# Matmuls with discarded results inside the last inverse transform and ahead of the first transposes

## The chip, the cores and the metric

The kernel runs on one core of a Trainium2 chip. The metric is the time of one execution on the device in microseconds. The engines are named as the profile names them: PE is TensorE (PEld its weight loads), ACT is ScalarE, DVE is VectorE, POOL is GpSimd, and SP issues most of the DMAs.

## The reference

A sequence of 2,048 positions with 640 channels passes two blocks, each modulated by vectors that come from `silu(c) @ w_mod`.

```python
h = layernorm(x) * (1 + ca) + sa
kv = shift_conv(k) * v                       # 4 taps along the sequence
y = causal_conv(kv, ssm_k) + kv * ssm_D      # the reference uses an FFT of length 4096
x = x + ga * (h * y)
h = layernorm(x) * (1 + cb) + sb
g = gelu(layernorm(h) @ w1)                  # w1 is 640 x 640
h1 = h + shift_quarters(g) @ w2              # quarters moved by +1, -1, +2, -2 positions
out = x + gb * (h1 + gelu(layernorm(h1) @ w3) @ w4)   # w3, w4: inner width 1728
```

All inputs and the output are bfloat16. The long convolution reaches over the whole sequence. The rest works position by position, apart from the small shifts ahead of w2.

## The kernel before, in words

The long convolution is done as a transform in matmuls. The 4,096-point transform is split in two stages (L408 and L425), once for the filter and once for `kv`. A product in the frequency domain and two inverse stages follow: `inverse1` (L617, L618) with the 128x128 matrices EA and EB, and `inverse2` (L658).

The sequence is held as 16 tiles of 128 positions. A tile A holds the positions whose remainder modulo 64 is 4A to 4A+3, so a position's neighbours in the sequence lie in the same tile or in the next one. `inverse2` takes groups of two or three tiles: [0,1,2], [3,4], [5,6,7], [8,9,10], [11,12,13] and [14,15]. For each tile it makes 32 small matmuls, 32 rows by 32 columns of the array with 160 moving columns each: four row blocks j4, four column blocks cg, and two accumulation steps cpp. Row blocks 0 and 1 go to the first PSUM slot of the group, 2 and 3 to the second. One task stands for the whole group, and two evacuations, on ACT (L209) or DVE (L211), copy the two slots to `y_all`.

Each tile then goes through `chain_a` (multiply by the modulated query, residual, sums for the layernorm), `chain_b` (the second block's layernorm and modulation) and `chain_c` (the inner layernorm and a transpose). The square sums are on ACT (L726). The reciprocal square roots are on POOL (L709, L712). The transpose is done in `turn`: for the first tiles on PE (L769, five 128x128 blocks into a PSUM slot `ps_tr`, which ACT L775 or DVE L777 copies out), and for all others as a DMA transpose issued by SP (L762). `pe_c` and `pe_m` set which: ten tiles go through PE, five ahead of w1 and five ahead of w3. `mm_w1` (L815, L825), `mm_w2` (L870), `mm_w3` (L904) and `mm_w4` (L934, L925) are the four matrix products, and each is evacuated by ACT (gelu) or DVE.

The order of all work is fixed. The kernel records about 1,075 tasks, and the string `ORDER` lists them with their engine and, for PE tasks, the PSUM slot or slots (four slots of 4 KB a partition). The engines then get their instructions in that order, each a queue that is worked off first to last. The groups of `inverse2` stand in PE's order as [0,1,2], two tasks of `silu(c) @ w_mod` (L483), [3,4], [14,15], [5,6,7], [8,9,10], the first tile's transposes, [11,12,13], and then the first w1 product. The cost figures in the calls of `add` were for a planner that made `ORDER`; with `ORDER` given they change nothing. An entry such as `498P:01` places task 498, the group [3,4], on PE with the slots 0 and 1.

Of the kernel before, what the change touches and what calls it, by code (L numbers as in the profile page):

```python
# [9 lines left out]
F32 = mybir.dt.float32  # L10
# [71 lines left out]
class Planner:  # L82
# [9 lines left out]
    def add(self, eng, cost, fn, r=(), w=(), lat=0.0, alloc=None, use=None, after=(), kb=0.0, rate=330.0, port=0.0, act=1.0, ni=0):  # L92
        t = Task()
        t.no = len(self.tasks)
        t.eng, t.cost, t.fn, t.lat, t.kb, t.rate, t.port, t.act, t.ni = eng, cost, fn, lat, kb, rate, port, act, ni
        t.alloc, t.frees = (() if alloc is None else alloc if isinstance(alloc, tuple) else (alloc,)), use
        deps = set(after)
        for acc, wr in [(a, False) for a in r] + [(a, True) for a in w]:
            reg, lo, hi = acc[:3]
            grp = acc[3] if len(acc) > 3 else None  # L100
            lst = self.acc.setdefault(reg, [])
            keep = []
            for e in lst:
                elo, ehi, ewr, egrp, et = e
                if elo < hi and lo < ehi and (wr or ewr) and not (wr and ewr and grp is not None and grp == egrp):
                    deps.add(et)
                if wr and grp is None and lo <= elo and ehi <= hi:
                    continue
                keep.append(e)
            self.acc[reg] = keep  # L110
        for acc, wr in [(a, False) for a in r] + [(a, True) for a in w]:
            self.acc[acc[0]].append((acc[1], acc[2], wr, acc[3] if len(acc) > 3 else None, t))
        deps.discard(t)
        t.deps = deps
        t.succ = []
        t.on = None
        for d in deps:
            d.succ.append(t)
        self.tasks.append(t)
        return t  # L120
# [18 lines left out]
def kernel(  # L139
# [4 lines left out]
    nc = tc.nc  # L144
# [11 lines left out]
    add = pl.add  # L156
# [5 lines left out]
    T01 = mem.tile([P, 20480], BF, name="T01")  # L162
    R3 = mem.tile([P, 20480], BF, name="R3")
    R5 = mem.tile([P, 20560], BF, name="R5")
    RG = mem.tile([P, 8192], BF, name="RG")
    RH = mem.tile([P, 4096], BF, name="RH")
# [30 lines left out]
    def ca(n):  # L197
        return 0.17 + 0.00083 * n
# [7 lines left out]
    def evac(dst, src, n, ps, w, eng=("ACT", "DVE")):  # L206
        def f(e):
            if e == "ACT":
                nc.scalar.copy(dst, src(ps.tile))  # L209
            else:  # L210
                nc.vector.tensor_copy(dst, src(ps.tile))  # L211
        return add(eng, {"ACT": ca(n), "DVE": cd(n)}, f, (), w, use=ps)

    def pst(ps, shape=None, dt=F32, name="ps"):
        if ps.tile is None:
            ps.tile = psA.tile(shape or [P, 2, 512], dt, name=name, tag="q" + ps.place)
        return ps.tile
# [119 lines left out]
    for kb in range(2):  # L337
# [9 lines left out]
        else:  # L347
# [3 lines left out]
            r=[wk[:3]], w=[wk], port=0.4)  # L351
# [9 lines left out]
        r=[("skT", 0, 1)], w=[("RQ", 0, 2560)], port=0.5)  # L361
# [72 lines left out]
    def dep(t, *on):  # L434
        for o in on:
            if o not in t.deps:
                t.deps.add(o)
                o.succ.append(t)

    for b in range(ND):  # L440
        add(("POOL", "DVE"), {"POOL": 0.2, "DVE": 0.16}, lambda e, b=b: eng_of[e].tensor_tensor(sT[:, b, 0:1], sT[:, b, 0:1], Dcol[:, b:b + 1], ALU.add),
            r=[("Dcol", 0, 1)], w=[("Ra", 2048 * b, 2048 * b + 2048)])
# [121 lines left out]
    for js in range(4):  # L564
        for jd in range(4):
            dma(("SP", "POOL"), 64, lambda q, js=js, jd=jd: q.dma_start(RH[32 * jd:32 * jd + 32, 1024 * js:1024 * js + 1024], RK[32 * js:32 * js + 32, 3072:4096]),
                r=[("RK", 3072, 4096)], w=[("RH", 1024 * js, 1024 * js + 1024, "h")], rate=215.0)
# [26 lines left out]
    EAf, EBf = (E[:].rearrange("p c n -> p (c n)") for E in (EA, EB))  # L594
# [41 lines left out]
    for g in range(4):  # L636
        dma("SP", 60, lambda q, g=g: q.dma_start(w2_sb[32 * g:32 * g + 32, 4, :], B_w2[160 * g + P:160 * g + 160, :]), w=[("RG", 3200, 6400, "w2")])
    add("POOL", 0.8, lambda e: nc.gpsimd.tensor_copy(w1x.rearrange("p b (g r) -> p b g r", g=4), w1_sb.rearrange("p b (g r) -> p b g r", g=4)[:, :, :, P:160]),
        r=[("RG", 0, 3200)], w=[("RG", 6400, 7040)])
# [6 lines left out]
    def inverse2(tilesA):  # L646
        n = len(tilesA)
        pss = [Slot() for _ in range(2)]

        def f(e):  # L650
            for s in pss:
                pst(s, name="ps_i2")
            for a, A in enumerate(tilesA):
                for j4 in range(4):
                    for cg in range(4):
                        n1 = 4 * A + cg
                        for cpp in range(2):
                            nc.tensor.matmul(pss[j4 // 2].tile[32 * cg:32 * cg + 32, j4 % 2, a * 160:(a + 1) * 160],  # L658
                                             lhsT=Hs[32 * j4:32 * j4 + 32, n1, cpp, :],
                                             rhs=Zb[32 * j4:32 * j4 + 32, cpp * 64 + n1, :, :],  # L660
                                             start=(cpp == 0), stop=(cpp == 1), tile_position=(32 * j4, 32 * cg))
        t1 = add("PE", 0.38 * n, f, r=[("T01", 0, 20480), ("RH", 0, 4096)], alloc=tuple(pss), act=0.2, ni=64 * n)
        yv = y_all[:, tilesA[0]:tilesA[0] + n, :].rearrange("p a (j u) -> p j a u", j=4)
        for i in range(2):
            t2 = evac(yv[:, 2 * i:2 * i + 2], lambda t: t[:, :, 0:160 * n].rearrange("p j (a u) -> p j a u", a=n), 320 * n, pss[i],
                      [("Rb", D * tilesA[0], D * (tilesA[0] + n), "y")])
            dep(t2, t1)
# [91 lines left out]
    def turn(dT, dk, src, sk, i, pe):  # L759

        if not pe:
            add("SP", 1.3, lambda e: nc.sync.dma_start_transpose(dT[:, :, i * P:(i + 1) * P], src), r=[sk], w=[dk + ("t",)], lat=1.6)  # L762
            return
        ps = Slot()

        def f(e):
            pt = pst(ps, [P, 2, 8, P], BF, name="ps_tr")
            for b in range(ND):
                nc.tensor.transpose(pt[:, 0, b, :], src[:, b * P:(b + 1) * P], ident)  # L769
        t0 = add("PE", 0.29, f, r=[sk, ("RG", 7680, 7808)], alloc=ps, act=0.2, ni=10)  # L770

        def f(e):
            o, x = dT[:, :, i * P:(i + 1) * P], ps.tile[:, 0, 0:ND, :]
            if e == "ACT":
                nc.scalar.copy(o, x)  # L775
            else:
                nc.vector.tensor_copy(o, x)  # L777
        t1 = add(("ACT", "DVE"), {"ACT": ca(640), "DVE": 0.47}, f, w=[dk + ("t",)], use=ps)
        dep(t1, t0)

    def chain_c(g, rn):
        hT, hTk = hnT[g % 3]
        for i, A in enumerate(CG[g]):
            hn, hk = hnr[A % 4]
            normed(hn, hk, h_all[:, A, :], hk_(A), rn, i)
            turn(hT, hTk, hn, hk, i, g < pe_c)
# [73 lines left out]
    def mm_w2(g):  # L860
        for t in MG[g]:
            ps = Slot()
            ix = m_idx[t]

            def f(e, ps=ps, t=t):
                pt = pst(ps, name="ps_w2")
                for fb in range(5):
                    for hf in range(2):
                        c0 = 64 + P * t - (32 * SH[fb] if fb < 4 else 0)
                        nc.tensor.matmul(pt[:, hf, 0:320], lhsT=gsf[:, fb, c0:c0 + P], rhs=w2_sb[:, fb, 320 * hf:320 * hf + 320],  # L870
                                         start=(fb == 0), stop=(fb == 4))
            r = [("gs", max(0, t - 1), min(NT, t + 2)), ("gx", t + 1, t + 2)]
            if t in (0, NT - 1):
                r += [("gpad", 0, 2)]
            t0 = add("PE", 1.37, f, r=r + [("RG", 3200, 6400)], alloc=ps, ni=20)
            hv = h_all[:, t, :].rearrange("p (a n) -> p a n", a=2)
            t1 = add("DVE", 0.82, lambda e, ps=ps, hv=hv, ix=ix: nc.vector.scalar_tensor_tensor(  # L877
                hv, ps.tile[:, :, 0:320], 1.0, hv, ALU.mult, ALU.add, accum_out=stat[:, 2, 0, ix:ix + 1]),
                w=[hk_(t), ("s1", 200 + ix, 201 + ix)], use=ps)
            dep(t1, t0)  # L880
            square_sum(h_all[:, t, :], hk_(t), 2, ix)
        rn = ln_finish(2, m_idx[MG[g][0]], len(MG[g]), g < quick_m)
        xT, xTk = xnT[g % 3]
        for i, t in enumerate(MG[g]):
            xn, xnk = xnr[m_idx[t] % 3]
            normed(xn, xnk, h_all[:, t, :], hk_(t), rn, i)
            turn(xT, xTk, xn, xnk, i, g < pe_m)
# [80 lines left out]
    def last_tile(t, pss, ta, tb):  # L968
# [6 lines left out]
        for hf, td in ((0, ta), (1, tb)):  # L975
# [6 lines left out]
            for cg in range(4):  # L982
                qe = ("SP", "ACT")[cg % 2] if hf else "SP"
                add(qe, 0.45, lambda e, cg=cg, qe=qe, c=c: (nc.sync if qe == "SP" else nc.scalar).dma_start(out_pos[4 * t + cg][:, c], o[32 * cg:32 * cg + 32, c]),
                    r=[oh], lat=1.6)

    inverse2([0, 1, 2])
    inverse2([3, 4])
    gs_zero()
    rest = [[5, 6, 7], [8, 9, 10], [11, 12, 13], [14, 15]]  # L990
    for tl in rest:
        inverse2(tl)
# [69 lines left out]
```

## Time and profile before

| | |
|---|---|
| median of 3 runs | 309.21 us (309.16 to 311.48) |
| profiled execution, its own time | 308.55 us |
| its span, first to last instruction | 306.6 us |
| mean granted PE clock | 0.956 |
| PE busy | 273.5 us (89%), 2,926 matmuls |
| DVE busy | 218.9 us (71%) |
| ACT busy | 210.4 us (69%) |
| POOL busy | 115.4 us (38%) |
| L658, the small matmuls of `inverse2` | 102.3 to 119.6 us of the span |
| L769, transposes on PE | 117.3 to 158.3 us, 50 matmuls |

The profile is of one execution. All its times are counted from the span's start, in microseconds. The row of PE's clock gives the share of full speed that was granted in each of 40 slices of 7.7 us. An idle time is shown with what ended it: the instruction on another engine that released the wait, or "issue" where the profile shows nothing that was waited for. The starts of matmuls are measured, and their ends are modelled.

### The profile page before, as it was taken

Reading aid. Unit: us, or ns where it says so; the run is one execution under the profiler, and the core shown is the slowest. Engines: PE = TensorE matmul, PEld = TensorE weight load, DVE = VectorE, ACT = ScalarE, POOL = GpSimd, SP = SyncE. Lnnn points to the kernel's source line nnn. Section 1 sums busy time; section 2 is a strip of 40 time slices with the busy share of each in tenths; the row PEclk is TensorE's granted clock in tenths of the full one; section 3 lists DMA queues with packets and bytes.
Section 4 is the critical chain, followed back from the end, with each engine's and each line's share of the span. In section 5 each row is a group of like instructions: output and inputs, shape, how many; then the busy total and the mean of one; then the engine's idle time right before and its main releaser. Section 6 shows DMA issues by size and latency. Waiting matters only on the chain.

```text
span 306.6 us, 7417 instructions
## 1 busy us (share of the span) xinstructions
PE 273.5 (89%) x2926; PEld 206.6 (67%) x2926; DVE 218.9 (71%) x430; ACT 210.4 (69%) x359; POOL 115.4 (38%) x257
## 2 busy tenths in 40 slices
PE   0999999996899757877999989999999899999992
PEld 0655556753888535856888767688867777897761
DVE  8999999999999998887689763924759135032342
ACT  4789999988689789998896686376643673542100
POOL 5898075052113698544337521424113130300000
PEclk9999999999799955599999999999999999999997
DMA  6999999669799942502800240222420402151112
GB/s 206 268 179 186 222 181 258 165 171 257 198 255 290 281 109 66 239 2 45 287 6 0 25 80 18 53 50 48 40 63 4 86 2 48 25 68 34 43 48 58
DMA packets 58163, 35.74 MB, mean 117 GB/s; under 512 B 39872, under 2 KB 54848, under 8 KB 58128
## 3 DMA queue, kind: packets, MB, share of 16 engines
q1 hardware_dynamic: 56896, 31.81, 44.8%
q0 software_dynamic: 1136, 3.41, 4.2%
q8 instruction: 23, 0.38, 0.5%
q14 instruction: 12, 0.10, 0.1%
q10 hardware_dynamic: 96, 0.04, 0.1%
HBM read 16.31 MB, written 2.62 MB: 62 GB/s over the span
## 4 chain that ended last, share of the span: by engine, by line
PE 50%; DVE 14%; ACT 10%; POOL 10%; DMA 7%; issue 6%; SPq 0%; ACTq 0%; POOLq 0%; DVEq 0%
PE ps_w L934 13%; PE ps_w L904 13%; PE ps_s L425 5%; PE ps_w L870 4%; PE ps_s L408 4%; PE ps_ksh L457 4%; POOL lnv L712 3%; DMA R<-RK 3%; PE ps_w L815 3%; DVE Rb L606 3%; DMA RG<-R 3%; ACT RG L726 2%; ACT R L209 2%; DVE Rb L395 2%; DMA Ra<-in_A_ssm_k_dram 1%
## 5 line engine op out<-in xcount | busy, mean ns | idle before, releaser
L904 PE MATMUL ps_w<-R,T 128*128 128x256 bf16 (+1 forms) x630 | 64.0, 261 | 0.0
L904 PEld LDWEIGHTS <-T 128*128 128x128 bf16 x630 | 55.8, 98 | 7.4 <-issue 1.3
L934 PE MATMUL ps_w<-T,R 128*128 128x320 bf16 x416 | 59.0, 299 | 0.0
L934 PEld LDWEIGHTS <-R 128*128 128x128 bf16 x416 | 40.3, 98 | 15.4 <-issue 0.3
L908 ACT ACTIVATE R<-ps_w 128x1024 bf16<-128x1024 f32 (+2 forms) x36 | 28.9, 826 | 28.6 <-PE ps_w L904 28.5
L726 ACT ACTIVATE RG<-R 128x640 bf16<-128x640 bf16 x32 | 23.5, 734 | 18.5 <-DVE R L753 10.1
L209 ACT CAST T<-ps_s 128x1024 bf16<-128x1024 f32 x33 | 31.6, 1025 | 3.5 <-PE ps_s L408 3.4
L957 DVE TENSOR_TENSOR T<-ps_w,R 128x640 bf16<-128x640 f32 x15 | 12.3, 822 | 27.7 <-PE ps_w L934 16.5
L408 PE MATMUL ps_s<-F1bd,Rb 128*128 128x256 bf16 x160 | 22.9, 295 | 8.8 <-DVE Rb L395 8.4
L408 PEld LDWEIGHTS <-Rb 128*128 128x128 bf16 x160 | 16.6, 106 | 15.0 <-DVE Rb L395 9.0
L877 DVE SCALAR_TENSOR_TENSOR R<-ps_w,R 128x640 bf16<-128x640 f32 x16 | 13.0, 818 | 17.8 <-PE ps_w L870 14.7
L209 ACT CAST R<-ps_s 128x640 bf16<-128x640 f32 x37 | 23.4, 722 | 1.9 <-PE ps_s L425 1.8
L617 PE MATMUL ps_i<-EA,Rb 128*128 128x128 bf16 x160 | 20.6, 227 | 3.1 <-DVE Rb L606 2.7
L712 POOL TENSOR_TENSOR lnv<-lnv,mhalf 128x2 f32<-128x2 f32 (+1 forms) x29 | 22.5, 776 | 2.3
L870 PE MATMUL ps_w<-RG,R 128*128 128x320 bf16 x160 | 23.1, 299 | 0.0
L425 PE MATMUL ps_s<-T,RG 64*128 64x320 bf16 x256 | 22.3, 297 | 0.3 <-ACT R L209 0.2
L209 ACT CAST T<-ps_i 128x1024 bf16<-128x1024 f32 x20 | 19.1, 1021 | 4.9 <-PE ps_i L618 4.8
L618 PE MATMUL ps_i<-EB,Rb 128*128 128x128 bf16 x160 | 20.4, 227 | 1.4 <-DVE Rb L606 1.4
L815 PE MATMUL ps_w<-R,RG 128*128 128x256 bf16 (+1 forms) x200 | 21.5, 273 | 0.0
L211 DVE CAST R<-ps_s 128x640 bf16<-128x640 f32 x27 | 20.7, 818 | 0.9 <-ACT R L209 0.2
L815 PEld LDWEIGHTS <-RG 128*128 128x128 bf16 x200 | 18.7, 110 | 1.6 <-issue 0.2
L711 POOL TENSOR_TENSOR lnv<-stat,lnv 128x2 f32<-128x2 f32 x19 | 5.5, 291 | 37.1 <-ACT RG L726 36.5
(173 smaller groups left out, 522.7 us busy)
## 6 DMA issues: line engine op xcount, KB each, us to landing
Ra<-in_A_ssm_k_dram SPq DMA_DIRECT2D x5, 512.0 KB, 5.5
Ra<-in_A_q_dram SPq DMA_DIRECT2D x8, 320.0 KB, 5.8
R<-in_w_mod_dram SPq DMA_DIRECT2D x6, 400.0 KB, 8.0
out_dram<-RH SPq DMA_DIRECT2D x60, 40.0 KB, 1.6
T<-in_B_w_dram SPq DMA_DIRECT2D x1, 2160.0 KB, 8.3
T<-in_B_w_dram SPq DMA_DIRECT2D x1, 2080.0 KB, 10.2
RH<-in_w_mod_dram SPq DMA_DIRECT2D x4, 400.0 KB, 5.1
RK<-R POOLq DMA_DIRECT2D x5, 256.0 KB, 5.1
```

Source lines behind the costliest of these rows:

```text
L209: nc.scalar.copy(dst, src(ps.tile))
L211: nc.vector.tensor_copy(dst, src(ps.tile))
L408: nc.tensor.matmul(psv[:, ml, :], lhsT=xL[:, s0:s0 + P], rhs=F1r, start=True, stop=True)
L425: nc.tensor.matmul(psv[:, g], lhsT=Gs[p, k, 64 - 64 * cc:192 - 64 * cc], rhs=T1b[p, cc * 32 + k], start=(cc == 0), stop=(cc == 1), tile_po ...
L617: nc.tensor.matmul(psv[:, w, :], lhsT=Av[:, r_, :, g_], rhs=EAf, start=True, stop=False)
L712: nc.gpsimd.tensor_tensor(rs, rs, mhalf[:, 0:n], ALU.pow)
L726: add("ACT", 0.74, lambda e: nc.scalar.activation(junk, src, ACT.Square, scale=float(D) ** -0.5, accum_out=stat[:, li, 1, t:t + 1]), r=[sk ...
L815: nc.tensor.matmul(pt[:, fb, 0:cw], lhsT=w1_sb[:, b, 160 * fb:160 * fb + P], rhs=hT[:, b, 0:cw], start=(b == 0), stop=(b == ND - 1))
L870: nc.tensor.matmul(pt[:, hf, 0:320], lhsT=gsf[:, fb, c0:c0 + P], rhs=w2_sb[:, fb, 320 * hf:320 * hf + 320], start=(fb == 0), stop=(fb == 4))
L904: nc.tensor.matmul(pt[:, fl, 0:cw], lhsT=w3_sb[:, b, fb * P:(fb + 1) * P], rhs=xT[:, b, 0:cw], start=(b == 0), stop=(b == ND - 1))
L908: nc.scalar.activation(g3[g % 2][:, f0:f0 + fn, 0:cw], ps.tile[:, 0:fn, 0:cw], ACT.Gelu_apprx_tanh)
L934: nc.tensor.matmul(bank(i, hf), lhsT=gg[:, fb, i * P:(i + 1) * P], rhs=w4_sb[:, fb, 320 * hf:320 * hf + 320], start=(fb == 0 and i == 0), ...
```

## The change

In `inverse2`, after row blocks j4 = 0, 1 and 2 of each tile, one matmul is added with all 128 rows and columns of the array: weights EA, moving data from T01, results into the last quarter of the group's second PSUM slot, from column 160 a to 512 for the a-th tile of the group. Row block 3 of the same tile and of the later tiles overwrites those columns, so nothing of the result is used. These are 48 matmuls with 512, 352 or 192 moving columns. In `turn`, on the PE path, three matmuls of 512 columns with the weights EA go to the unused half of the transposes' PSUM slot, ahead of the five transposes. These are 30 for the ten tiles. The recorded reads grow by what the new matmuls read. `ORDER` stays as it is, and so do the order of all other instructions on every engine and the number of instructions on the engines other than PE.

```diff
+                    if j4 < 3:
+                        nc.tensor.matmul(pss[1].tile[:, 1, 160 * a:512], lhsT=EAf, rhs=T01[:, 160 * a:512], start=True, stop=True)
-        t1 = add("PE", 0.38 * n, f, r=[("T01", 0, 20480), ("RH", 0, 4096)], alloc=tuple(pss), act=0.2, ni=64 * n)
+        t1 = add("PE", 0.38 * n, f, r=[("T01", 0, 20480), ("RH", 0, 4096), ("E", 0, 1)], alloc=tuple(pss), act=0.6, ni=70 * n)
...
             pt = pst(ps, [P, 2, 8, P], BF, name="ps_tr")
+            spare = pt[:, 1].rearrange("p b n -> p (b n)").bitcast(F32)
+            for _ in range(3):
+                nc.tensor.matmul(spare, lhsT=EAf, rhs=RG[:, 0:512], start=True, stop=True)
             for b in range(ND):
                 nc.tensor.transpose(pt[:, 0, b, :], src[:, b * P:(b + 1) * P], ident)
-        t0 = add("PE", 0.29, f, r=[sk, ("RG", 7680, 7808)], alloc=ps, act=0.2, ni=10)
+        t0 = add("PE", 0.29, f, r=[sk, ("RG", 7680, 7808), ("RG", 0, 512), ("E", 0, 1)], alloc=ps, act=0.2, ni=16)
```

## Prediction

> **What bounds the kernel now.** First the page's slices of the span and the total waits of TensorE (PE):
>
> ```profile
> PE   0999999996899757877999989999999899999992
> ...
> PEclk9999999999799955599999999999999999999997
> PE ps_i L658 <- issue: 5.3, 3, 1.9
> PE ps_tr L769 <- DVE RK L721: 2.6, 3, 1.4
> ```
>
> One stretch, slices 14 to 17, has little PE work and half a clock; the 32x32 matmuls of the last inverse (L658) lie there and stand idle three times, with no releaser in the trace. Next the order of PE's work there (start, duration, idle before it):
>
> ```profile
> 102.34 1.21 PE L658 MATMUL ps_i<-T,RH 32*32 32x160 bf16 x96
> 103.48 1.53 PE L483 MATMUL ps_mod<-R,silu_w 128*128 128x320 bf16 x10
> 104.94 0.35 PE L658 MATMUL ps_i<-T,RH 32*32 32x160 bf16 x16
> 105.45 0.29 PE L658 MATMUL ps_i<-T,RH 32*32 32x160 bf16 x2 [0.16 <-DVE Rb L211]
> 107.43 2.34 PE L658 MATMUL ps_i<-T,RH 32*32 32x160 bf16 x128 [1.68 <-issue]
> 111.43 2.10 PE L658 MATMUL ps_i<-T,RH 32*32 32x160 bf16 x128 [1.67 <-issue]
> 115.43 1.00 PE L658 MATMUL ps_i<-T,RH 32*32 32x160 bf16 x46 [1.91 <-issue]
> 117.33 0.71 PE L769 MATMUL ps_tr<-RG,RK 128*128 128x128 bf16 x5 [0.89 <-DVE RK L721]
> 117.97 1.64 PE L658 MATMUL ps_i<-T,RH 32*32 32x160 bf16 x96
> 119.54 2.31 PE L815 MATMUL ps_w<-R,RG 128*128 128x128 bf16 x20
> ...
> 148.34 0.44 PE L769 MATMUL ps_tr<-RG,RH 128*128 128x128 bf16 x5
> ```
>
> A tile has 32 of these matmuls, so the groups can be counted off: tiles [0,1,2] at 102.34; [3,4] from 104.94 to 108.00; then [14,15], [5,6,7], [8,9,10] until 116.43; [11,12,13] at 117.97. The idle times come after exactly 128 weight-load and matmul pairs, 256 instructions, and PE resumes every 4.00 us: it waits for its instructions.
>
> What waits for these groups is ScalarE (ACT), which empties their PSUM (L209). Its queue in order of time:
>
> ```profile
> 108.00 1.29 ACT L209 CAST Rb<-ps_i 128x640 bf16<-128x640 f32 x2 [0.99 <-PE ps_i L658]
> 109.91 1.28 ACT L209 CAST Rb<-ps_i 128x640 bf16<-128x640 f32 x2
> 116.47 0.96 ACT L209 CAST Rb<-ps_i 128x960 bf16<-128x960 f32 x1 [0.26 <-PE ps_i L658]
> 120.71 2.66 ACT L209 CAST Rb<-ps_i 128x960 bf16<-128x960 f32 x3
> 123.39 1.28 ACT L817 ACT_TABLE_LOAD   x1
> ```
>
> From 120.71 to 135.2 ACT has only gaps of 0.2 us, none of them put down to PE, and the chain of waits runs through it. Before that (110.17 to 118.9) the chain is GpSimd's (POOL) layernorm steps, first released by ACT's square sum, which is queued behind the 108.00 evacuation. So an inverse group that ends later is felt, and a faster matmul between 117 and 129 us, where every consumer is late anyway, is not. From 145.6 us on PE is full except for two DMA-transpose waits of 0.94 (183.45) and 0.89 (241.71).
>
> **The skill.** "TensorEngine Tiling (Array Packing)", Key Properties: changing the tiling mode drains the engine. The trace agrees and prices it: the 26 matmuls of L934 from 169.88 start every 0.136, so the last starts at 173.28, and the 64-row one behind it at 173.51: 0.23, or 0.095 more. From the last 32x32 start of the first group (103.32) to the full-array one at 103.48 it is 0.160: 160 columns (0.067) and 0.093. At half clock the same step before 119.54 takes 0.269, some 0.136 more than the columns.
> "TensorE: Matmul & The Clock Gate", What's actually happening: a 3,413 ns free-running window judges activity; an idle one halves the clock, a busy one restores it. Narrow stretches of the table by stretch show half clock from 108.8 to 129.27, six such windows. Same page, Back-to-back issue gap: columns over 2.4 GHz plus 2.5 ns; the 0.136 for 320 columns agrees.
> "Runtime: NRT & Kernel Launch", Instruction fetch mechanics: refills come in blocks of 256 instructions and are mostly hidden. The block size agrees; hidden they are not (5.3 us).
>
> **Part 1: 48 matmuls within the inverse groups.** After row blocks 0 to 2 of each tile stands one 128x128 matmul of 512, 352 or 192 columns (first, second, third tile of the group). Each changes the mode twice. One costs columns/2.4 + 0.19 us: 0.40, 0.34, 0.27; thrice each, 1.2, 1.0, 0.8. So a group of three tiles takes 1.14 + 3.0 = 4.15, one of two 0.76 + 2.2 = 3.0. Bounds of the unseen mixture: no drain at all (1.3 and 1.1 per group), or twice the drain. I take the measured drain, because three kinds of pairs show the same 0.095.
> Now the walk, each step as time before -> after:
> - [0,1,2] ends 103.5 -> 106.5; the ten w_mod matmuls behind it 104.9 -> 108.0.
> - [3,4]: its instructions are there at 107.43, so the first fetch wait vanishes under the delay. Ends 108.0 -> 111.0 (+3.0). ACT's evacuation, the square sum behind it and POOL's 110.17 step move as much. VectorE's own half of the first group (104.25) moves by 2.3 and is no later than that.
> - [14,15] ends at 114.0, ACT wanted it at 109.91 + 3.0: ACT now +4.1.
> - [5,6,7] ends at 118.1, ACT wants it at 114.41 + 4.1 = 118.5: nothing. A block of instructions now lasts over 4 us, so the other two fetch waits are gone too; without that cover this would be 3.6 worse.
> - [8,9,10] ends at 122.3, ACT wants it at 116.47 + 4.1 = 120.6: ACT +5.9.
> - the first transposes with their extras (0.75) until 123.4, then [11,12,13] until 127.7; ACT wants it at 120.71 + 5.9 = 126.6: ACT +7.0.
> From there ACT is in order and full, and the transposes on DMA that PE waits for at 145.61 come out of it: +7.0. The extras also write the second PSUM slot from the first block on instead of the third; it is free by then in each group (the slot's evacuations are the ACT rows above).
>
> **Part 2: 30 matmuls of 512 columns ahead of ten tiles' transposes.** They do not read the tile that the transposes wait for, only the weights and a free slot. Three take 3 x 0.216 = 0.65, with no mode change. Before 146 us: PE waits there for VectorE (0.4 to 1.4 us each), and with the clock kept they fit; the pair at 130.83 would exceed its 0.65 wait once, but PE's consumers run 7 us late then. Cost nothing; without that cover 0.65 each. At 148.34 and 149.18 PE is full: +1.3, also for ACT's rows that follow (155.8). The pair at 157.80: +1.3, of which the 0.94 wait at 183.45 can take most: +0.4 to +1.3. Sum 1.7 to 2.6, taken 2.0.
>
> **What the clock brings.** The window before the fall at 108.8 holds 118 small matmuls, that is 118 x 160 / 16 columns of the whole array, 0.5 of 3.4 us or 14%; the one before an earlier fall at 78.1 holds 1,920 columns, 23%. From 142.9 to 146.3 there are 3,584 columns, 44%, and the clock stays:
>
> ```profile
> 105.40:108.80 3.40, 1.67 (x120) 1.26 (x125) 3.30 (x9) 1.72 (x3) 1.40 (x3) 1.00 1.07 208
> 108.80:112.20 3.40, 1.64 (x81) 0.86 (x83) 2.93 (x5) 3.37 (x8) 3.07 (x4) 0.50 0.55 144
> 142.90:146.30 3.40, 1.71 (x26) 1.50 (x24) 1.85 (x9) 1.99 (x6) 2.31 (x7) 1.00 0.63 111
> ```
>
> The columns are time, then busy time of PE, weight loads, VectorE, ACT, POOL, then clock. Busy time is alike in the first and the last, yet only one fell; array columns tell them apart. A new group of three streams (3,168 + 960) / 2,400 = 1.72 of 4.15 us, 41%; one of two 45%. I expect the clock to hold, and to gain nothing, for the reason above.
>
> **Sum.** The profiled execution took 308.55 (span 306.6 and 1.95 around it): + 7.0 + 2.0 = 317.55. The median of the runs is 309.21, 0.66 higher: 318.2.
>
> **Rivals.**
> - *The insertions are nearly free* (tiles and full matmuls overlap without drain, fetch waits hide the rest): [3,4] ends near 109.1, later groups are in time for ACT; about +1.3, with part 2 +3.4: 312.6. For it: 5.3 us of fetch waits lie open. Against: the drains measured.
> - *The clock falls all the same* (the change doesn't do what it says). An insertion then costs columns/1.2 + 0.27, a group of three 6.7, one of two 4.9. From [14,15] on: 115.9, 122.6, 129.3, transposes 131.5, then 138.2, where ACT wanted 120.7: +17.5, in all about 329; less if it falls later. It decides whether the limit lies above 41%; it lies between 23 and 44.
> - *Not slower: the full clock pays.* Some 9,900 columns of full-array work run at half clock between 117.3 and 129.3, 8.2 us for 4.1. If PE, and not ACT, set the pace there, 4.1 would come back, against 2.0 of part 2, with the fetch waits taking part 1: 307.1. It decides wherever ACT shows idle time released by PE; between 120.7 and 135.2 it shows none.
>
> **Chances.** Clock held, drains paid: 60% (own range 314.5 to 322). Nearly free 15%. Clock falls 15%. Not slower 10%. The range leaves out the last and the upper half of the fall: 310.5 to 327. A measurement of this kernel tells about 1% from no change, so 306.1 to 312.3: faster 0.06, within 0.11, slower 0.83.
>
> **What would show it.** Start-to-start 0.16 before and columns/2.4 + 0.095 after each insertion; no wait without a releaser on L658; groups of 4.15 and 3.0; clock 1.0 from 108 to 130; ACT's evacuation at 120.71 moved to about 127.7; PE's wait at 145.61 moved by about 7, and the final part longer by 2. It would be wrong if insertions follow the small matmuls without a drain, if the clock drops, or if ACT makes up time before 145 us.

## Result and the profile after

The changed kernel takes 325.37 us in the median of four executions, against 309.19 for the kernel before. The four are 320.1, 323.2, 327.5 (the profiled one) and a stray 1,013. The ratio is 1.039, 95% interval 1.029 to 1.049. A second set of eight executions on another chip gave 1.033 (1.028 to 1.038). Both ratios leave out the executions more than 1.5% above the fastest, here the last two and there the four slower ones. The change makes the kernel slower by 3 to 4%, and by 5 to 6% in the executions in which the clock falls.

The executions of the second set are of two kinds, which the mean granted clock of PE tells apart: four took 319.2 to 320.0 us at a mean clock of 0.989 to 0.993, and four took 324.3 to 327.3 at 0.954 to 0.965. In the first set 320.1 (0.989) and 327.5 (0.965) fit these kinds, and 323.2 (0.971) lies between them. The profile below is of the slower kind (327.53 us, span 325.6). Of the faster kind there is no trace; by estimate, a mean of 0.989 over 318 us leaves about 7 us at half clock in all, so it can't have had the 20.5 us that the profile shows in this stage.

The page's slices after the change, PE's busy share and its clock:

```profile
PE   0999998995889999998889999999999999999994
...
PEclk9999999999999995579999999999999999999998
```

PE is now busy all through the stage, and the clock falls anyway, later than before: at 121.7 us in place of 108.8, and until 142.2. Now the order of PE's work there (start, duration, line, operands, count). A row of 16 small matmuls holds the last eight of one tile and the first eight of the next:

```profile
103.95 0.33 PE L658 MATMUL ps_i<-T,RH 32*32 32x160 bf16 x8
104.21 0.10 PEld L663 LDWEIGHTS <-EA 128*128 128x128 bf16 x1
104.21 0.39 PE L663 MATMUL ps_i<-T,EA 128*128 128x512 bf16 x1
104.53 0.33 PE L658 MATMUL ps_i<-T,RH 32*32 32x160 bf16 x8
...
108.88 1.53 PE L483 MATMUL ps_mod<-R,silu_w 128*128 128x320 bf16 x10
110.34 0.33 PE L658 MATMUL ps_i<-T,RH 32*32 32x160 bf16 x8
...
113.64 0.35 PE L658 MATMUL ps_i<-T,RH 32*32 32x160 bf16 x16
...
116.97 0.35 PE L658 MATMUL ps_i<-T,RH 32*32 32x160 bf16 x16
...
121.67 0.49 PE L658 MATMUL ps_i<-T,RH 32*32 32x160 bf16 x16
122.09 0.61 PE L663 MATMUL ps_i<-T,EA 128*128 128x512 bf16 x1
...
129.34 1.46 PE L772 MATMUL ps_tr<-RG,EA 128*128 128x512 bf16 x3
...
138.92 2.31 PE L820 MATMUL ps_w<-R,RG 128*128 128x128 bf16 x20
```

The first group goes from 103.95 to 108.88, 4.93 us where it had 1.14. A row block with a 512-column insertion takes 0.58 (103.95 to 104.53). The last small matmul ahead of the insertion starts at 104.05, and the insertion's own weight load (LDWEIGHTS) only at 104.21, with the insertion: so the extra wait lies ahead of the weight load and is not the load itself. Groups of two take 3.4 (110.34 to 113.75, eight small matmuls into the row at 113.64). At half clock [8,9,10] takes 7.6, up to the transposes' matmuls at 129.34, and [11,12,13] takes 7.65, from 131.27 to 138.92. No wait without a releaser is left on these matmuls. ACT's evacuations of the groups, with the idle time ahead of each and who ended it, answer the rows shown before:

```profile
109.01 0.96 ACT L209 CAST Rb<-ps_i 128x960 bf16<-128x960 f32 x1 [4.53 <-PE ps_i L658]
113.01 0.69 ACT L209 CAST Rb<-ps_i 128x640 bf16<-128x640 f32 x1 [1.50 <-PE ps_i L658]
...
117.37 1.29 ACT L209 CAST Rb<-ps_i 128x640 bf16<-128x640 f32 x2 [1.91 <-PE ps_i L658]
...
121.87 1.80 ACT L209 CAST Rb<-ps_i 128x960 bf16<-128x960 f32 x2
...
129.48 0.96 ACT L209 CAST Rb<-ps_i 128x960 bf16<-128x960 f32 x1 [5.81 <-PE ps_i L658]
139.08 2.68 ACT L209 CAST Rb<-ps_i 128x960 bf16<-128x960 f32 x3 [5.43 <-PE ps_i L658]
141.78 1.28 ACT L822 ACT_TABLE_LOAD   x1
```

ACT, which had waited 2.0 us for the small matmuls in all of this stage, now waits 19.5. Counted from the first small matmul, its table load has moved from 21.05 (102.34 to 123.39) to 37.83 (103.95 to 141.78), by 16.8 us. The profiled execution is longer by 19.0. Of the rest, 1.6 us lie ahead of the first small matmul, where nothing was added, and 0.6 behind the table load: so the loss is made in this stage. The table by stretch shows the fall of the clock (time, then PE, weight loads, VectorE, ACT, POOL, clock, DMA share, GB/s):

```profile
114.90:118.30 3.40, 3.40 (x79) 1.44 (x78) 2.54 (x7) 1.49 (x4) 2.43 (x4) 1.00 0.02 5
118.30:121.70 3.40, 3.40 (x84) 1.51 (x79) 2.44 (x7) 3.31 (x8) 2.24 (x5) 1.00 0.00 0
121.70:125.10 3.40, 3.40 (x53) 1.01 (x52) 2.28 (x5) 1.97 (x4) 2.98 (x8) 0.50 0.02 5
```

PE has work at every moment of the stretch before the fall. Counted in columns of the whole array, as in the prediction, that stretch streams 34% of what it could, and the two before it 40%.

### The profile page after: what moved, and what is told of

Read it like the earlier page. It is cut to its first block, busy times and chain, and to the rows that moved or that the text cites. A ratio compares the mean times of both kernels' runs of the same rounds, so it can differ in the third digit from the quotient of the medians.

```text
span 325.6 us, 7570 instructions
## 1 busy us (share of the span) xinstructions
PE 299.3 (92%) x3004; PEld 211.9 (65%) x3004; DVE 219.5 (67%) x430; ACT 211.0 (65%) x359; POOL 111.6 (34%) x257
## 4 chain that ended last, share of the span: by engine, by line
PE 51%; DVE 13%; ACT 8%; POOL 8%; DMA 7%; SPq 7%; issue 5%; ACTq 0%; DVEq 0%; POOLq 0%
PE ps_w L909 13%; PE ps_w L939 12%; DVE Rb L606 5%; SPq L235 5%; PE ps_i L658 5%; PE ps_i L663 5%; PE ps_w L875 4%; PE ps_w L820 3%; ACT RG L728 3%; DMA R<-in_A_v_dram 2%; POOL lnv L714 2%; PE ps_mod L483 2%; DMA Ra<-in_A_ssm_k_dram 2%; ACT R L209 2%; PE ps_s L425 2%
## 5 line engine op out<-in xcount | busy, mean ns | idle before, releaser
L617 PE MATMUL ps_i<-EA,Rb 128*128 128x128 bf16 x160 | 19.3, 219 | 3.5 <-DVE Rb L606 3.5
L209 ACT CAST Rb<-ps_i 128x960 bf16<-128x960 f32 (+1 forms) x11 | 9.1, 863 | 19.5 <-PE ps_i L658 19.5
L714 POOL TENSOR_TENSOR lnv<-lnv,mhalf 128x2 f32<-128x2 f32 (+1 forms) x29 | 20.7, 715 | 2.3
L618 PE MATMUL ps_i<-EB,Rb 128*128 128x128 bf16 x160 | 19.0, 219 | 2.3 <-DVE Rb L606 2.2
L457 PE MATMUL ps_ksh<-R,RQ 128*128 128x512 bf16 x80 | 18.9, 379 | 1.5 <-DVE R L462 1.5
```

Of the source, the lines that this page charges most:

```text
L617: nc.tensor.matmul(psv[:, w, :], lhsT=Av[:, r_, :, g_], rhs=EAf, start=True, stop=False)
L618: nc.tensor.matmul(psv[:, w, :], lhsT=Bv[:, r_, :, g_], rhs=EBf, start=False, stop=True)
L714: nc.gpsimd.tensor_tensor(rs, rs, mhalf[:, 0:n], ALU.pow)
```

## Experiments

Three explanations compete: the mode changes (each insertion pays two, and ACT passes the delay on), the streamed columns alone, and the fall of the clock alone. Ratios are to the kernel before on the same chip.

**Part 1 alone.**

```diff
-            for _ in range(3):
-                nc.tensor.matmul(spare, lhsT=EAf, rhs=RG[:, 0:512], start=True, stop=True)
```

> The 48 insertions within the inverse groups alone; nothing ahead of the transposes. Drain theory (each insertion costs its columns and two mode changes, and the evacuations on ACT pass it on): the profile of the changed kernel shows groups of three at 4.9 us and of two at 3.4 us with the full clock, so 317 to 319 us while the clock holds, up to 325 when it falls between 115 and 125 us. Columns theory (only the streamed columns count, 1.3 and 1.1 us a group, and the fetch waits hide most): 310 to 311. Clock theory (the loss is the fall to half clock alone): 309 where the clock holds, and the loss of the changed kernel only where it falls.

Measured: 323.17 us (321.8 to 323.4), ratio 1.041 (1.036 to 1.046). Part 1 alone makes the whole loss. It is as slow as both parts together, not 2 us faster. A likely reason, not tested by itself, is its clock: it fell in all four executions (mean 0.962 to 0.972, in the profile from 128.8 to 139.0 us), where with both parts it held in half of the second set.

**The same columns, without the mode changes.**

```diff
+            for a in range(n):
+                for _ in range(3):
+                    nc.tensor.matmul(pss[1].tile[:, 1, 160 * a:512], lhsT=EAf, rhs=T01[:, 160 * a:512], start=True, stop=True)
             for a, A in enumerate(tilesA):
...
-                    if j4 < 3:
-                        nc.tensor.matmul(pss[1].tile[:, 1, 160 * a:512], lhsT=EAf, rhs=T01[:, 160 * a:512], start=True, stop=True)
```

> The same 48 matmuls with the same columns, but all of a group ahead of its first small matmul: one or two mode changes a group in place of 18 or 12. Drain theory: a group of three takes 1.14 + 1.32 + 0.2 = 2.7 us, one of two 2.0; the first group delays ACT by little, later ones lie in the fetch waits: 309.8 to 311. Columns theory: the same time as with the insertions spread out. Clock theory: if the clock then stays full from 108 to 129 us and a full clock is worth something there, below 309; if it is worth nothing, not below.

PE's first groups in its profile; L655 are the extra matmuls, of which the trace kept eight of nine and five of six, and L661 the small ones:

```profile
102.28 1.51 PE L655 MATMUL ps_i<-T,EA 128*128 128x512 bf16 x8
103.71 1.20 PE L661 MATMUL ps_i<-T,RH 32*32 32x160 bf16 x96
104.85 1.53 PE L483 MATMUL ps_mod<-R,silu_w 128*128 128x320 bf16 x10
106.22 1.26 PE L655 MATMUL ps_i<-T,EA 128*128 128x512 bf16 x5
107.41 0.88 PE L661 MATMUL ps_i<-T,RH 32*32 32x160 bf16 x64
```

A group of three now takes 2.57 us (102.28 to 104.85) with the same streamed columns for which it takes 4.93 when they are spread. Measured: 312.35 us, ratio 1.008 (1.005 to 1.010). Four fifths of part 1's loss go when the columns stand together, so the columns theory is out. What goes is the mode changes, and with them the fall of the clock that part 1 alone had late in the stage. The time is 1.4 us above the drain theory's upper end, and 0.8 of this is the chip, where the kernel before takes 310.0. In the profile ACT's table load comes only 0.9 us later than before, counted from PE's first matmul of the stage (102.28 to 124.20); from there to the end it is 2.4 us longer. The clock stayed full from 80.8 to 132.0 us, but then fell twice for 3.4 us where the kernel before kept it, the second time at 149.0: the twenty w1 matmuls from 148.27 take 3.72 us, where their like took 2.35 (146.15). So a full clock through the whole stage did not shorten the stage.

**The mode changes, without the columns.**

```diff
-                        nc.tensor.matmul(pss[1].tile[:, 1, 160 * a:512], lhsT=EAf, rhs=T01[:, 160 * a:512], start=True, stop=True)
+                        nc.tensor.matmul(pss[1].tile[:, 1, 160 * a:160 * a + 16], lhsT=EAf, rhs=T01[:, 160 * a:160 * a + 16], start=True, stop=True)
```

> The 48 insertions in their places, with 16 columns each in place of 512, 352 or 192: the mode changes without the streaming. Drain theory: each costs 0.27 us at full and 0.40 at half clock (the last small matmul's 0.067 that is no longer overlapped, and 0.093 and 0.107 for the two changes), groups of 3.6 and 2.4, at half clock 5.2 and 3.5; the clock falls near 108.8 as before: ACT's last evacuation 7 to 9 us later, 316 to 318. Columns theory: 16 columns are 7 ns, no change, 309.2 to 309.6. Clock theory: no change either, as the clock falls as before.

```profile
103.48 0.33 PE L658 MATMUL ps_i<-T,RH 32*32 32x160 bf16 x8
103.74 0.18 PE L663 MATMUL ps_i<-T,EA 128*128 128x16 bf16 x1
103.85 0.33 PE L658 MATMUL ps_i<-T,RH 32*32 32x160 bf16 x8
```

A row block takes 0.37 us (103.48 to 103.85), where eight small matmuls at the old rate (1.14 / 96 each) take 0.095: an insertion of next to no work costs 0.28. Measured: 318.83 us, ratio 1.027 (1.021 to 1.033), as the drain theory had it: 0.8 us over its upper end on a chip where the kernel before takes 310.0, and 317.6 by the ratio on 309.2. The clock fell at 106.0 us, a little earlier than before, and stayed at half until 136.7, ten us longer in all, so this run alone does not exclude the clock theory. What excludes it is that the row blocks above cost 0.28 more at full clock, and that the faster executions of the changed kernel, at a mean clock of at least 0.989, take 10 us more than the kernel before, which has 0.950 to 0.971.

**One insertion in place of three.**

```diff
-                    if j4 < 3:
+                    if j4 == 2:
```

(nothing ahead of the transposes)

> One insertion per tile, after the third row block, in place of three; nothing ahead of the transposes. If a cost per insertion reached the end as it stands, a third of what part 1 costs alone: +4.2, 313.5. If PE's fetch waits and ACT's own backlog take up what comes first (groups longer by 1.3 and 0.9 us, fetch restarts at 107.4, 111.4 and 115.4 as before): ACT's evacuations 0.7 us later at [3,4] and not more after that, 309.9 to 310.7.

Measured: 309.83 us, ratio 0.997 (0.994 to 1.000). Sixteen insertions cost nothing, 48 cost 4%. ACT's table load comes 21.85 us after the first small matmul (103.75 to 125.60), 0.8 later than before, and of the fetch waits one of 2.0 us is left (112.66). The first part of the cost lies in waits that were there anyway. In this profile half clock also lasts shorter, 13.7 us in place of 20.5; what that gave back was not measured by itself.

**One group alone.**

```diff
-                    if j4 < 3:
+                    if j4 < 3 and tilesA[0] == 11:
```

> Insertions in the group [11,12,13] alone, nine of the 48. This group has no fetch wait, and ACT wants it 1.1 us after PE's end. At half clock, as in the kernel before at this place, it takes 8.1 us in place of 1.65: ends at 126.1, 5.4 us after ACT is free: 314 to 315. At full clock 3.3 longer: +2.5, 311.7. If a late evacuation here were made up by ACT before 145 us: 309 to 310.

ACT's evacuation of this group and the table load behind it:

```profile
126.62 2.68 ACT L209 CAST Rb<-ps_i 128x960 bf16<-128x960 f32 x3 [4.55 <-PE ps_i L658]
129.32 1.28 ACT L820 ACT_TABLE_LOAD   x1
```

Measured: 313.87 us, ratio 1.009 (1.007 to 1.012), so about 2.9 us for nine of the 48 insertions; the expectation at half clock was 5. Counted from ACT's first evacuation of the stage the table load is at 24.31 in place of 19.78 (before: 103.61 to 123.39), 4.5 later. So ACT is as late as expected within a microsecond, and a part is made up before the end: 0.9 us in this profile (182.3 us from the table load to the end, before 183.2), 1.6 by the ratio.

**Part 2, whole and in halves.** Whole, the 48 insertions are taken out. For the halves:

```diff
-            for _ in range(3):
+            for _ in range(3 if sk[0] == "RK" else 0):
```

with "RK" for the first five tiles (ahead of w1) and "RH" for the second five (ahead of w3).

> The 30 matmuls ahead of the ten transposes alone. Drain theory: no mode changes here, five of the ten are hidden in PE's waits before 146 us, the others cost 1.7 to 2.6 us: 310.9 to 311.8. The clock falls near 108.8 us as before. Were the ones ahead of the first five transposes on the path as well: 313 to 315, more at half clock.

> The three matmuls ahead of the transposes of the first five tiles only (those ahead of w1). The prediction's step: all five fall into PE's waits before 146 us: 309.2, no change (up to +0.6 if half clock makes the second and third too long for their waits). Rival, PE's order matters there: +1.5 to 2 and the last five nothing.

> The three matmuls ahead of the transposes of the second five tiles only (those ahead of w3). The prediction's step: one hidden, two at 0.65 us each on a full PE, and the pair at 157.8 of which the DMA wait at 183 us can take 0.94: +1.7 to 2.6, so 310.9 to 311.8. Rival: the layernorm chain, not PE, sets the pace there: 309.2.

> All 30 matmuls ahead of the ten transposes again, on the chip of the others here. The two halves alone gave -1.1 and +0.4 us. If they add up: 308.5 to 309.0. If the first measurement (+2.1) holds: 311, and the halves are not independent.

Measured: whole 1.007 (1.0045 to 1.0089) on one chip and 1.003 (0.9996 to 1.006) on another; first five 0.996 (0.994 to 0.998); second five 1.001 (0.9995 to 1.003). The first five gain a little over 1 us where I expected nothing, and the second five cost at most 1 us where I expected 1.7 to 2.6. PE's waits for DMA transposes after 160 us, in the profile of the second five, are one place where it can have gone; the kernel before had 0.94 and 0.89 there:

```profile
187.43 0.71 PE L828 MATMUL ps_w1x<-R,RG 128*128 128x256 bf16 x5 [0.17 <-DMA R<-RK]
244.96 0.71 PE L828 MATMUL ps_w1x<-R,RG 128*128 128x256 bf16 x5 [0.16 <-DMA R<-RK]
```

Both waits are shorter, by 1.5 together, and a new one of 0.44 stands at 274.00. I had let only the first of them take anything. This does not show the cause, as the wait at 241.71 is also gone in the profile of the first five, which adds nothing there. In the two profiles of the whole part 2, ACT's table load is where it was (21.05 and 21.06 us after the first small matmul) and from there to the end it is 2.1 and 2.0 us longer, which is the predicted cost. In that of the second five it is 0.9 longer; but the load comes 0.9 later too, with nothing added ahead of it, so single profiles differ by that much. Whether the halves add up is not settled: -1.1 and +0.4 against +2.1 and +0.8 for the whole.

**The two parts again**, on the chip of the halves:

> The changed kernel once more, beside the next three on one chip. Drain theory with the group lengths seen since (4.9 and 3.4 us at full clock): the walk gives ACT's last evacuation 10 us late and 2 us from the transposes: 320 to 322 with the clock held, 3 to 6 more where it falls from 121 us on. If the two parts add up as measured alone (12.6 and 2.1): 324. If part 2 hides behind part 1's delay: 322, as part 1 alone.

Measured: the two kinds given at the top, 319.2 to 320.0 and 324.3 to 327.3.

**Half of the small matmuls.**

```diff
-                        for cpp in range(2):
+                        for cpp in range(1):
...
-                                             start=(cpp == 0), stop=(cpp == 1), tile_position=(32 * j4, 32 * cg))
+                                             start=True, stop=True, tile_position=(32 * j4, 32 * cg))
```

> The kernel before, with the second accumulation step of every small matmul pair of the last inverse left out, so that half of that product is missing from the output; the groups have half the instructions. Fetch theory: PE's waits without releaser again come after multiples of 128 pairs and end 4.0 us apart, now one or two in place of three; tiles [3,4] end near 105.4 in place of 108.0. If that first wait is on the path as the chain of waits has it, 307.5; but POOL's own queue is busy until 110.0 and ACT's square sum is only 0.17 later, so at most a few tenths: 308.6 to 309.2.

Measured: 308.97 us, ratio 1.000 (0.998 to 1.002). The fetch waits are gone altogether, where I expected one or two, and the time is the same. So the 1.68 us wait at 107.43, which the chain of waits of the kernel before names, was worth nothing that this measurement could see: with half of the matmuls ACT takes the tiles [3,4] without waiting for PE, only 0.5 us sooner than before (3.88 us behind its first evacuation, before 4.39). This also supports that the fetch waits were slack that insertions could use.

**A version for the gaps.** Extra matmuls where PE waits anyway: ahead of three groups, and ahead of the first five transposes.

```diff
+            for _ in range(3 if tilesA[0] in (14, 5, 8) else 0):
+                nc.tensor.matmul(pss[1].tile[:, 1, 0:512], lhsT=EAf, rhs=T01[:, 0:512], start=True, stop=True)
             for a, A in enumerate(tilesA):
...
+            for _ in range(3 if sk[0] == "RK" else 0):
+                nc.tensor.matmul(spare, lhsT=EAf, rhs=RG[:, 0:512], start=True, stop=True)
```

> Three matmuls of 512 columns ahead of the groups [14,15], [5,6,7] and [8,9,10], where PE waits for instructions anyway, and the three ahead of each of the first five transposes; no insertions within a group. If a kept clock is worth a little and the rest hides in the waits: below the 307.8 that the first five alone gave, 306.5 to 307.5. If the kept clock is worth nothing: 308 to 309.5, as the groups may come up to 1 us late at ACT.

Measured: 309.51 us, ratio 0.9955 (0.993 to 0.998), no better than the first five transposes alone. By the ratio this is 307.8 on 309.2, between the two expectations. Both are some 0.4% under the kernel before. In both profiles half clock lasts shorter in the stage: 6.8 us here and 13.7 with the five transposes, 20.5 before. That the shorter fall is the cause was not tested by itself, and it is not enough: the two profiles of the whole part 2 have 13.7 and 10.2 us, and that kernel is not faster.

## Why the prediction was right, and where its steps were off

The time (318.2) and the range (310.5 to 327) held: 320.1 and 323.2 lie in it, as do 319.2 to 320.0 and three of the five executions in which the clock fell (324.3 to 327.5). The likeliest case, drains paid and ACT late, is the one that the runs show. That the number is so near is in part luck: the insertions were priced some 3 to 4 us too low in all, part 2 some 1.5 to 2 us too high, and the clock was a bet at 60%.

- *Mode changes*: right as mechanism, and decisive: 1.041 spread out, 1.008 in front with the same columns, 1.027 with hardly any columns. The **term was too small**. I took 0.40 us for an insertion of 512 columns, from columns and two changes of 0.095. The trace has 0.58 for the row block less 0.095 for its small matmuls, 0.485. Left out was the streaming of the last small matmul (0.067), which lies bare once nothing overlaps it. The change back to small matmuls costs 0.107 behind a lone insertion, not 0.095. A group of three took 4.93 us in place of 4.15, one of two 3.4 in place of 3.0.
- *The walk to ACT*: the shape was right. ACT waits for PE ahead of each group's evacuation but that of [5,6,7] (121.87), the one for which the walk had no wait. The walk's last step doesn't add up: 122.3, 0.75 and 4.15 make 127.2 and not 127.7, so ACT +6.5 in place of +7.0. With 4.9 and 3.4 in the walk ACT takes [5,6,7] about 6 us late in place of 4.1; counted from the first small matmul, the profile has 5.9. The last evacuation would then be about 10 us late, and the sum about 321, where the faster executions took 319.2 to 320.1. The difference fits **the 2.0 us of part 2, which don't show in the changed kernel**: from ACT's table load to the end its two profiles, both with the fallen clock, take 0.6 and 0.0 us more than before. The step "from there ACT is in order and full: +7.0" held: with part 1 alone the table load is 12.6 us later, and the way from there to the end 0.1 longer. With one group alone 0.9 us were made up.
- *Fetch waits*: right that they vanish under the longer groups. The runs with a third of the insertions and with half of the matmuls show that they were slack.
- *Part 2*: "cost nothing" before 146 us was right, but for a small gain. The 1.7 to 2.6 us after it are what the profiles of the whole part 2 show, but **too much for the second five alone** (at most 1 us) and for the changed kernel. Why the cost differs stays open.
- *The clock*: **"I expect the clock to hold" is true of about half the executions**, four of eight in the second set. I argued with 41% of streamed columns between a share that fell (23%) and one that held (44%). In this stage 40% held and 34% fell; but with the extra matmuls in front a later window with 41% fell too (145.6 to 149.0 us), so a share of columns does not settle it. The rival price of 329 was for a fall from the third group on; in the profile it fell at 121.7, with the fifth group, and the executions in which it fell took 324.3 to 327.5. "To gain nothing" may be off by about 1 us: in the second set, executions of the kernel before with a mean clock of at least 0.965 took 308.7 us on average, and those under 0.960 took 310.0. On the two other chips the same difference is 1.1 and 0.4 us. This is a correlation and not an experiment.
- *Nearly free* is refuted for 48 insertions and true for 16. *Not slower* falls with the changed kernel itself, which takes 10 us more where its clock is kept, and with the kernel that kept a full clock through the stage and was not shorter there.

## What to carry to other kernels

Before adding work to an engine that looks idle, ask which of its waits are slack and how much of them the addition uses: 16 insertions were free here and 48 cost 4%. On TensorE price the change of tiling mode, about 0.1 us each way plus the streaming of the last small matmul, ahead of the columns, and put full-array work at a border between groups. What a full clock is worth depends on who waits for PE: 4 to 8 us in the changed kernel, where ACT waited, and nothing that could be seen in the same stage with the extra matmuls in front.

## What the runs showed of the hardware that was not expected

- The clock fell after a window in which PE was busy throughout (118.3 to 121.7 us, 3.40 of 3.40) with small matmuls and insertions in turn. Busy time as the profile counts it, with modelled ends, did not keep the clock.
- The same program takes 319 to 320 or 324 to 327 us, and its mean clock goes with it (at least 0.989, at most 0.965). With part 1 alone it fell in all four executions; with part 2 added, which only adds work, it held in four of eight, and the median was no longer (1.042 times the kernel before, as with part 1 alone). Four executions are too few to say that part 2 is what keeps the clock.
- The two changes of mode are not alike. At full clock the step into the full array costs 0.093 us beyond the columns (0.160 start to start in every such pair of the profile after), and the step back to 32x32 costs 0.107 behind a lone insertion and 0.096 behind the ten w_mod matmuls. At half clock it is 0.135 in and 0.110 back behind a lone insertion.
